# One weight block's last conversion step moved ahead of the next blocks' first step on VectorE, in a fused state-space and GELU kernel

## The chip, the cores and the metric

The kernel runs on one core of a Trainium2 chip. A core has a matrix engine (TensorE; PE in the profile, with its weight loads shown apart as PEld), two elementwise engines (VectorE, DVE in the profile; ScalarE, ACT in the profile), GpSimd (POOL) and SyncE (SP), which mostly starts transfers. Each engine works through its own instructions in order, and waits for others by semaphores. The metric is the device time of one execution in microseconds, lower is better; the time before is the median of three runs.

## The reference, cut to what matters

Two layers follow each other. The first is a chunked state-space scan over 4 sequences of 768 steps with 8 heads; its result is laid out as 3072 tokens of 256 numbers. The second is a two-layer network on these tokens, with a quick GELU between.

```python
    for c in range(nc):                       # chunks of 32 steps; la = log of the clipped a
        cum = np.cumsum(la, axis=-1)
        L = np.exp(cum[:, :, :, None] - cum[:, :, None, :]) * causal
        M = np.einsum('bhin,bhjn->bhij', Cc, Bc) * L
        y[:, :, sl] = np.einsum('bhij,bhjd->bhid', M, xc) \
            + np.einsum('bhin,bhnd->bhid', Cc, state) * np.exp(cum)[:, :, :, None]
        ...                                   # the state is decayed and added to
...
def _moe_ref(x, w_in, w_out) -> np.ndarray:   # x: 3072 x 256
    h = x @ w_in                              # w_in: 256 x 2048
    g = h * (1.0 / (1.0 + np.exp(-1.702 * h)))
    return (g @ w_out).astype(np.float32)     # w_out: 2048 x 256
...
    attn_out = _attn_ref(**attn_kwargs)
    x = np.ascontiguousarray(attn_out.transpose(0, 2, 1, 3)).reshape(B * S, H * D)
    return _moe_ref(x=x, **moe_kwargs)
```

The weights `moe_w_in` and `moe_w_out` are 64-bit floating-point numbers in memory. The kernel reads them as pairs of 32-bit words and makes 32-bit numbers of them itself.

## The kernel before

The 3072 tokens are worked in six groups of 512. For each group the scan gives `yT` (256 features by 512 tokens, two tiles of 128 rows), and the network multiplies it by the 16 column blocks of `w_in` (`w_in[:, f]`, 128 columns each, two halves of 128 rows) and then by the blocks of `w_out`. Group 0 is special: its hidden layer, `hidden(0, f)` for f = 0 to 15, runs while the weights are still being fetched and converted. From group 1 on the weights are all there.

**Conversion.** The weights come in pieces (`PIECES`, line 155): pieces 0 to 3 hold two blocks of `w_in` each, pieces 4 and 5 four blocks each, pieces 6 to 9 four blocks of `w_out` each. So piece 3 is blocks 6 and 7, and piece 4 is blocks 8 to 11. A piece passes through five steps:

- `fetch(i)` (line 164): two transfers from SyncE's queue (line 181).
- `fields(i)` (line 189): two VectorE instructions over the whole piece, which cut the exponent bits into `power[i]` (line 193, tile `p`) and the mantissa bits into `mantissa[i]` (line 196, tile `m`).
- `clamp(i)` (line 199): two ScalarE activations over `power[i]` (lines 204 and 205).
- `rounded(i)` (line 207): one VectorE instruction that adds the low word to the mantissa (line 209).
- `join(i, parts)` (line 216): for each part one VectorE instruction that puts the sign to the power (line 223) and one that multiplies mantissa and power into the weight tile (line 229). With `parts=2` the first half of the piece's blocks is finished before the second.

`narrow(i)` (line 236) orders this on VectorE: `rounded(i)`, then either `join(i)` or `fields(i + 1)` first. For pieces 2, 4, 5 and 6 `join(i)` stands first; for piece 3 `fields(4)` stands ahead of the whole of `join(3, 2)`.

**Hidden layer.** `hidden(g, f)` (line 869) takes a bank of PSUM from a pool of four (`bank`, line 563), issues the two matrix products of the block (line 878; each stands in the profile as two matmuls and two weight loads) and then one activation on ScalarE from that bank into `gT` (line 882). Block f takes the bank that block f - 4 had, so its first product waits for that block's activation.

The order of the program around the change is set by this table and loop; the work listed for f is issued right after `hidden(0, f)`:

```python
    for i, k, c in ((2, 1, 1), (3, 2, 2), (4, 4, 7), (5, 8, 10), (6, 10, 14), (7, 14, 15)):
        at(in_hidden[0], k, lambda i=i: narrow(i))
        at(in_hidden[0], c, lambda i=i: clamp(i + 1))
...
    for f in range(NF):
        hidden(0, f)
        for do in in_hidden[0].get(f, []):
            do()
```

So `narrow(3)` and `clamp(4)` are issued after `hidden(0, 2)`. On ScalarE the two activations of `clamp(4)` therefore stand between the activation of block 2 and that of block 3. `narrow(4)`, which makes blocks 8 to 11, is issued after `hidden(0, 4)`.

Of the kernel before, what the change touches and what calls it, by code (L numbers as in the profile page):

```python
# [35 lines left out]
def kernel(  # L36
# [122 lines left out]
    bits, pieces = {}, {}  # L159

    def words(name):
        return wide.tile([P, 2 * PN], U32, tag="bits", name=name, bufs=BUFS)

    def fetch(i, held=False):
        name, f, n = PIECES[i]
        if n == 2 and f % 4:
            t = pieces.pop(i - 1)[:, 2 * n * DM:]
        else:
            t = pieces[i] = words(f"bits{i}")
            t = t[:, :2 * n * DM]  # L170
        if held:
            held.memset(t[:, :1], 0)
        if name == "in":
            src = moe_w_in[:, 2 * f * P:2 * (f + n) * P].rearrange("(k p) e -> p k e", p=P)
            dst, src = (v.rearrange(s, h=n, e=2 * P) for v, s in (
                (t, "p (h k e) -> k p h e"), (src, "p k (h e) -> k p h e")))
        else:
            src = moe_w_out[f * P:(f + n) * P, :].rearrange("(f p) (h e) -> h p f e", p=P, h=2)
            dst = t.rearrange("p (h f e) -> h p f e", h=2, f=n)
        for k in range(2):  # L180
            nc.sync.dma_start(out=dst[k], in_=src[k])  # L181
        t = t.rearrange("p (e w) -> p e w", w=2)
        bits[i] = t[:, :, 0], t[:, :, 1]
# [3 lines left out]
    mantissa, power = {}, {}  # L187

    def fields(i):
        hi, cols = bits[i][1], slice(0, PIECES[i][2] * DM)  # L190
        mantissa[i] = wide.tile([P, PN], U32, tag="m", name=f"m{i}")[:, cols]
        power[i] = wide.tile([P, PN], U32, tag="p2", name=f"p2{i}")[:, cols]
        nc.vector.tensor_scalar(out=power[i], in0=hi, scalar1=0x7FF00000, scalar2=None,
                                op0=ALU.bitwise_and)

        nc.vector.tensor_scalar(out=mantissa[i], in0=hi, scalar1=0x000FFFFF,
                                scalar2=0x00100000, op0=ALU.bitwise_and, op1=ALU.bitwise_or)
# [9 lines left out]
    def rounded(i):  # L207

        nc.vector.scalar_tensor_tensor(out=mantissa[i].bitcast(FP32), in0=bits[i][0],
                                       scalar=2.0 ** -32, in1=mantissa[i],  # L210
                                       op0=ALU.mult, op1=ALU.add)


    NEXT = {1: (6,), 5: (9,)}

    def join(i, parts=1):

        name, f, n = PIECES[i]
        n //= parts
        low, m, p2 = bits.pop(i)[1], mantissa.pop(i), power.pop(i)  # L220
        for k in range(parts):
            cols, fs = slice(k * n * DM, (k + 1) * n * DM), slice(f + k * n, f + (k + 1) * n)
            nc.vector.scalar_tensor_tensor(out=p2[:, cols], in0=low[:, cols], scalar=0x80000000,
                                           in1=p2[:, cols], op0=ALU.bitwise_and, op1=ALU.bitwise_or)
            if name == "in":
                dst, h = w_in[:, fs].rearrange("p f k e -> p (f k e)").unsqueeze(1), 1
            else:
                dst, h = w_out[:, :, fs].rearrange("p c f e -> p c (f e)"), 2
            nc.vector.scalar_tensor_tensor(  # L229
                out=dst, in0=m[:, cols].bitcast(FP32).rearrange("p (h e) -> p h e", h=h),  # L230
                scalar=2.0 ** -20, in1=p2[:, cols].bitcast(FP32).rearrange("p (h e) -> p h e", h=h),
                op0=ALU.mult, op1=ALU.mult)
        for n in NEXT.get(i, ()):
            fetch(n)

    def narrow(i):
        rounded(i)
        if i in (2, 4, 5, 6):
            join(i, 2 if i in (4, 5) else 1)
        if i == 6:  # L240
            decay_rows(0)
        if i + 1 < len(PIECES):
            fields(i + 1)
        if i not in (2, 4, 5, 6):
            join(i, 2 if i == 3 else 1)


    scratch = dram.tile([NC, 2, NB * NH, H], FP32, name="scratch")
# [133 lines left out]
    for n in range(PG):  # L382
        t = whose[32 * n:32 * n + 32, n:n + 1]
# [115 lines left out]
    def decay_rows(b):  # L499

        t, first = raf.pop(b), firsts.pop(b)
        if b:
            since[b] = ssd.tile([P, NC, P], FP32, tag="since", name=f"since{b}")
        nc.vector.tensor_tensor_scan(
            out=since[b][:, -t.shape[1]:].rearrange("p c s -> p (c s)"), data0=t.rearrange("p c s -> p (c s)"),
            data1=first.rearrange("p c s -> p (c s)"),
            initial=0.0, op0=ALU.mult, op1=ALU.add)
# [686 lines left out]
    dense(8, bank("dense"))  # L1194
    finish(range(PG))
    join(0, 2)
    fold_ident(1)
    fields(1)
# [22 lines left out]
# [3 lines that stand above are left out]
# [3 lines left out]
    n, p = 2 * PG, 3 * PG  # L1227
# [5 lines left out]
       lambda: decay_rows(1))  # L1233
    at(in_project[0], 4, lambda: turn(PG + 1))
    at(in_project[0], 5, lambda: narrow(9))
    at(in_project[0], 10, lambda: score(pairs), lambda: gain(pairs), lambda: keep_both(pairs, True),
       lambda: weigh(PG), lambda: weigh(PG + 1))
# [90 lines left out]
    k = NF // 2 - 1  # L1328
# [6 lines left out]
    for g in range(2, NG):  # L1335
        n, p = (g + 1) * PG, (g + 2) * PG
# [60 lines left out]
        k = NF // 2 - 1  # L1397
# [42 lines left out]
```

## Time and profile before

| | |
|---|---|
| time before, median of 3 runs | 346.89 us (346.83 to 347.21) |
| the profiled execution's own time | 347.67 us |
| its span, first instruction to last | 345.9 us |
| TensorE busy (PE), share of the span | 339.2 us, 98% |
| VectorE busy (DVE) | 256.1 us, 74% |
| ScalarE busy (ACT) | 155.1 us, 45% |
| granted TensorE clock, mean | 1.0 |

A row of the timeline has a start in microseconds from the span's start, a length in microseconds, the engine, the line, the operation, the tile written and the tiles read with their shapes, and how many instructions it merges; a bracket gives the idle time ahead of it on its engine and what ended that. A row of the chain of waits has start, length and what the end of the program hung on then. A row of the list of waits has who waited for whom, the total in microseconds, how often, and the longest. The end of a matmul is modelled. "bits" is the tile of raw words, "p" the power, "m" the mantissa.

### The profile page before, as it was taken

How to read it: one execution, taken by the hardware profiler on the slowest of the kernel's cores; microseconds unless marked ns; L12 is line 12 of the kernel's file. 1: busy time of each engine (PE TensorE's matmuls, PEld its weight loads, DVE VectorE, ACT ScalarE, POOL GpSimd, SP SyncE). 2: the span in 40 equal slices, each digit the busy share in tenths (PEclk: the TensorE clock that was granted, in tenths of full speed). 3: DMA queues.
4: the chain of work that ended last, by engine and by line, in shares of the span. 5: the costliest groups of instructions: out<-in, count | busy, mean ns of one | idle time of the engine just before them, and what ended most of it. 6: DMA issues, size and time to landing. Idle time of an engine off the chain costs nothing.

```text
span 345.9 us, 8116 instructions
## 1 busy us (share of the span) xinstructions
PE 339.2 (98%) x3380; PEld 270.2 (78%) x3380; DVE 256.1 (74%) x484; ACT 155.1 (45%) x352; POOL 16.7 (5%) x40
## 2 busy tenths in 40 slices
PE   8999999999999999999999999999999999999996
PEld 6633744555788888888888888888888888899996
DVE  5988999999799998858995667787564654465463
ACT  5786771507454324754332554442454322554320
POOL 7300110300000100000000000000000000000000
PEclk9999999999999999999999999999999999999999
DMA  6698899545637100435603036400000300000401
GB/s 160 132 289 211 217 239 133 152 67 102 122 63 127 36 0 15 65 99 100 110 27 51 2 78 121 64 0 3 0 4 2 62 2 0 0 2 0 63 0 62
DMA packets 90004, 25.76 MB, mean 74 GB/s; under 512 B 73416, under 2 KB 87248, under 8 KB 89968
## 3 DMA queue, kind: packets, MB, share of 16 engines
q1 hardware_dynamic: 89104, 24.72, 35.0%
q10 hardware_dynamic: 832, 0.52, 0.5%
q8 instruction: 26, 0.43, 0.5%
q14 instruction: 10, 0.08, 0.1%
q0 software_dynamic: 32, 0.01, 0.0%
HBM read 22.00 MB, written 3.24 MB: 73 GB/s over the span
## 4 chain that ended last, share of the span: by engine, by line
PE 92%; DMA 3%; SPq 2%; DVE 1%; issue 0%; ACT 0%; POOL 0%; DVEq 0%
PE acc L1039 28%; PE X L934 19%; PE Y L944 14%; PE o L976 8%; PE acc L1046 7%; PE h L878 7%; DMA bits<-in_moe_w_in_dram 3%; PE y L818 2%; PE cb L664 2%; SPq L181 1%; PE y L804 1%; PE A L695 1%; PE ab L536 1%; DMA az<-in_a_dram 1%; POOL CsT L649 0%
## 5 line engine op out<-in xcount | busy, mean ns | idle before, releaser
L939 ACT ACTIVATE ac<-X 128x256 f32<-128x256 f32 x76 | 29.1, 383 | 81.7 <-PE X L934 81.0
L1039 PE MATMUL acc<-mg,mw 128*128 128x256 f32 x192 | 54.5, 379 | 0.0
L1066 DVE TENSOR_TENSOR gT<-Y,ac 128x512 f32<-128x512 f32 x38 | 26.2, 689 | 38.1 <-PE Y L944 32.5
L911 ACT ACTIVATE gT<-gT 128x512 f32<-128x512 f32 (+1 forms) x76 | 38.9, 519 | 29.3 <-DVE gT L1066 28.8
L934 PE MATMUL X<-my,mi 128*128 128x256 f32 x152 | 45.2, 380 | 0.0
L1039 PEld LDWEIGHTS acc<-mg,mw 128*128 128x128 f32 x192 | 36.6, 190 | 4.9
L1066 DVE TENSOR_TENSOR gT<-Y,b 128x256 f32<-128x256 f32 x38 | 15.8, 419 | 28.5 <-PE Y L944 28.5
L878 PE MATMUL h<-yT,w_in 128*128 128x512 f32 (+1 forms) x92 | 35.5, 541 | 1.4 <-DVE w_in L229 0.9
L1039 PE MATMUL acc<-gT,w_out 128*128 128x256 f32 x128 | 35.5, 380 | 0.0
L878 PEld LDWEIGHTS h<-yT,w_in 128*128 128x128 f32 x92 | 17.2, 190 | 18.2 <-issue 12.8
L934 PEld LDWEIGHTS X<-my,mi 128*128 128x128 f32 x152 | 28.0, 190 | 4.0 <-ACT ac L939 0.3
L976 PE MATMUL o<-gT,w_out 128*128 128x512 f32 x64 | 28.3, 596 | 0.0
L902 DVE TENSOR_TENSOR mg<-gT 128x512 f32<-128x512 f32 x40 | 27.2, 681 | 0.0
L1039 PEld LDWEIGHTS acc<-gT,w_out 128*128 128x128 f32 x128 | 24.3, 190 | 3.4 <-ACT yT L853 0.2
L939 ACT ACTIVATE b<-X 128x256 f32<-128x256 f32 x38 | 14.6, 383 | 20.8 <-PE X L934 20.3
L934 PE MATMUL X<-yT,w_in 128*128 128x256 f32 x76 | 23.2, 389 | 0.0
L944 PE MATMUL Y<-yT,w_in 128*128 128x256 f32 x76 | 22.7, 381 | 0.0
L944 PE MATMUL Y<-my,mi 128*128 128x256 f32 x76 | 22.7, 381 | 0.0
L934 PE MATMUL X<-my,w_in 128*128 128x256 f32 x76 | 22.5, 380 | 0.0
L944 PE MATMUL Y<-yT,mi 128*128 128x256 f32 x76 | 22.5, 380 | 0.0
L976 PEld LDWEIGHTS o<-gT,w_out 128*128 128x128 f32 x64 | 11.9, 190 | 13.6 <-issue 12.7
L408 DVE TENSOR_TENSOR_SCAN L<-a,idents 128x1024 f32<-128x1024 f32 x9 | 20.5, 2279 | 0.3 <-DMA a<-scratch 0.3
(152 smaller groups left out, 547.8 us busy)
## 6 DMA issues: line engine op xcount, KB each, us to landing
a<-scratch SPq DMA_DIRECT2D x18, 256.0 KB, 4.9
bits<-in_moe_w_out_dram SPq DMA_DIRECT2D x8, 512.0 KB, 7.4
x<-in_x_dram SPq DMA_DIRECT2D x24, 128.0 KB, 3.7
out_dram<-ob SPq DMA_DIRECT2D x40, 64.0 KB, 2.0
bits<-in_moe_w_in_dram SPq DMA_DIRECT2D x8, 256.0 KB, 3.7
bits<-in_moe_w_in_dram SPq DMA_DIRECT2D x4, 512.0 KB, 11.4
b<-in_B_dram SPq DMA_DIRECT2D x20, 64.0 KB, 3.3
af<-in_a_dram SPq DMA_DIRECT2D x3, 384.0 KB
```

The costliest lines, as they stand in the source:

```text
L408: nc.vector.tensor_tensor_scan(out=L, data0=ra[p].rearrange("p k e -> p (k e)"), data1=idents.rearrange("p h i -> p (h i)"), initial=0.0, ...
L664: nc.tensor.matmul(out=s["cb"][side, r, k].rearrange("p (q i) -> p q i", q=Q), lhsT=BT[rows, k, side], rhs=CT[rows, k, :, side], start=Tru ...
L878: nc.tensor.matmul(out=h[:, cols], lhsT=w_in[:, f, k], rhs=yT[g][:, k, cols], start=(k == 0 and c == 0), stop=(k == NK - 1), skip_group_ch ...
L902: nc.vector.tensor_tensor(out=t[:, 0:2], in0=B[:, :, 1], in1=B[:, 0], op=ALU.subtract)
L911: nc.scalar.activation(o, i, AF.Silu, scale=GELU_SCALE)
L934: nc.tensor.matmul(out=s["X"], lhsT=lhsT, rhs=rhs, start=i == "1", stop=i == "4", skip_group_check=True)
L939: nc.scalar.activation(copy, s["X"], AF.Copy)
L944: nc.tensor.matmul(out=o, lhsT=lhsT, rhs=rhs, start=s.pop("new", False), stop=i != "5", skip_group_check=True)
L976: nc.tensor.matmul(out=o[c], lhsT=w_out[:, c, f], rhs=gT[g, f // 2][:, f % 2], start=(f == 0), stop=(f == NF - 1), skip_group_check=True)
L1039: nc.tensor.matmul(out=acc[g][0][i][:, cols], lhsT=w, rhs=h[:, cols], start=(j == 0 and k == 0 and (i, 0) in begins), stop=(j == NF // 2 - ...
L1046: nc.tensor.matmul(out=o[k] if type(o) is list else o[:, cols], lhsT=h[:, cols], rhs=w, start=(j == 0 and (i, k) in begins), stop=(j == NF ...
L1066: nc.vector.tensor_tensor(out=o, in0=v, in1=w, op=ALU.add)
```

## The change

In `narrow(3)` the join is taken apart. Before, VectorE had `rounded(3)`, `fields(4)`, `join(3)` for block 6, `join(3)` for block 7. Now it has `rounded(3)`, `join(3)` for block 6, `fields(4)`, `join(3)` for block 7. `join` gets a parameter that names the parts to do, and keeps the piece's tiles until the last part is done. No instruction is added or removed: in the built program the lines 223 and 229 of block 6 (128x256 each) stand ahead of the lines 193 and 196 of piece 4 (128x1024 each) on VectorE, and the order on TensorE, ScalarE, GpSimd and SyncE is as before.

```diff
-    def join(i, parts=1):
+    def join(i, parts=1, only=None):
 
         name, f, n = PIECES[i]
         n //= parts
-        low, m, p2 = bits.pop(i)[1], mantissa.pop(i), power.pop(i)
-        for k in range(parts):
+        low, m, p2 = bits[i][1], mantissa[i], power[i]
+        for k in range(parts) if only is None else only:
             cols, fs = slice(k * n * DM, (k + 1) * n * DM), slice(f + k * n, f + (k + 1) * n)
...
-        for n in NEXT.get(i, ()):
-            fetch(n)
+        if only is None or parts - 1 in only:
+            for t in bits, mantissa, power:
+                t.pop(i)
+            for n in NEXT.get(i, ()):
+                fetch(n)
 
     def narrow(i):
         rounded(i)
...
+        if i == 3:
+            join(i, 2, (0,))
         if i + 1 < len(PIECES):
             fields(i + 1)
-        if i not in (2, 4, 5, 6):
-            join(i, 2 if i == 3 else 1)
+        if i == 3:
+            join(i, 2, (1,))
+        elif i not in (2, 4, 5, 6):
+            join(i)
```

## The prediction, as put on record before the changed kernel ran

> **What bounds the kernel now.** I read the page's chain of waits first, then the chain in order of time around the edit, then the timelines of VectorE, ScalarE and TensorE there, and last the list of waits after it.
>
> ```profile
> PE 92%; DMA 3%; SPq 2%; DVE 1%; issue 0%; ACT 0%; POOL 0%; DVEq 0%
> ...
> 17.15 9.61 DMA bits<-in_moe_w_in_dram
> ...
> 27.28 0.69 DVE p L193
> ...
> 28.95 0.44 DVE w_in L229
> ...
> 29.52 17.43 PE h L878 x52
> ```
>
> The end hangs on TensorE for 92% of the span. The other pieces of the chain lie in the first 29.5 us: the last of them runs from the landing of piece 4's words (17.15 + 9.61 = 26.76) over `fields(4)` and the join of block 6 to TensorE. From 29.52 on TensorE hangs on nothing but itself; of its matmuls after 30 us the list of waits has only the row of this same wait:
>
> ```profile
> PE h L878 <- DVE w_in L229: 0.9, 1, 0.9
> ```
>
> So TensorE's beat set at 29.5 us is carried to the end, and the question is how much earlier it can be. VectorE there:
>
> ```profile
> 25.49 0.69 DVE L209 SCALAR_TENSOR_TENSOR m<-bits,m 128x512 f32<-128x512 uint32 x1
> 27.28 0.69 DVE L193 TENSOR_SCALAR p<-bits 128x1024 uint32<-128x1024 uint32 x1 [1.10 <-DMA bits<-in_moe_w_in_dram]
> 27.89 0.69 DVE L196 TENSOR_SCALAR m<-bits 128x1024 uint32<-128x1024 uint32 x1
> 28.49 0.42 DVE L223 SCALAR_TENSOR_TENSOR p<-bits,p 128x256 uint32<-128x256 uint32 x1
> 28.95 0.43 DVE L229 SCALAR_TENSOR_TENSOR w_in<-m,p 128x256 f32<-128x256 f32 x1
> 29.29 0.42 DVE L223 SCALAR_TENSOR_TENSOR p<-bits,p 128x256 uint32<-128x256 uint32 x1
> ```
>
> Block 6 (lines 223 and 229 at 28.49 and 28.95) stands behind piece 4's fields, and these stand idle 1.10 us for their transfer. ScalarE and TensorE's weight loads:
>
> ```profile
> 25.91 0.72 ACT L205 ACTIVATE p<-p,edge 128x512 uint32<-128x512 f32 x1
> 26.53 0.58 ACT L882 ACTIVATE gT<-h 128x512 f32<-128x512 f32 x1
> 28.01 1.15 ACT L204 ACTIVATE p<-p,edge 128x1024 f32<-128x1024 uint32 x1 [0.90 <-DVE p L193]
> 29.19 1.15 ACT L205 ACTIVATE p<-p,edge 128x1024 uint32<-128x1024 f32 x1
> 30.24 2.04 ACT L882 ACTIVATE gT<-h 128x512 f32<-128x512 f32 x4
> ```
>
> ```profile
> 27.65 0.19 PEld L878 LDWEIGHTS h<-yT,w_in 128*128 128x128 f32 x1 [0.24 <-issue]
> 29.49 0.30 PEld L878 LDWEIGHTS h<-yT,w_in 128*128 128x128 f32 x2 [1.65 <-ACT p L204]
> ...
> 30.89 0.19 PEld L878 LDWEIGHTS h<-yT,w_in 128*128 128x128 f32 x1 [0.24 <-ACT gT L882]
> ...
> 32.75 0.47 PEld L878 LDWEIGHTS h<-yT,w_in 128*128 128x128 f32 x2 [0.38 <-issue]
> ```
>
> Two things are to be seen. The load at 27.65 is block 5's last; at a beat of 0.43 the next would come at 28.08, and comes at 29.49. And the load at 30.89, block 7's first, is released by an activation of line 882: block 7 takes the PSUM bank of block 3, whose activation is the first of the four at 30.24, behind `clamp(4)`, which waits for piece 4's line 193. It ends at 30.24 + 0.58 = 30.82. In the kernel before, TensorE comes to block 7 just as that bank is freed. That is a second gate right behind the first, and the edit doesn't move it forward.
>
> **The change, part by part.** Nothing is added or removed; two pairs of VectorE instructions change places. No transfer is issued by either, and no queue but VectorE's is reordered.
>
> *Block 6 forward.* Line 223 of block 6 waits for `clamp(3)`'s line 205, which ends at 25.91 + 0.72 = 26.63; after such an end it starts 0.03 later (the same timelines: line 205 at 22.61 for 0.72, line 223 at 23.36, for piece 2): 26.66. Line 229 follows 0.46 later (28.49 to 28.95), at 27.12, and ends at 27.55. TensorE's load follows 0.11 after such an end (29.38 to 29.49), at 27.66, before the beat of 28.08. So the wait at block 6 goes. Its price: after a wait the second load of a block follows the first by 0.11 (two loads of 0.19 in 0.30), so block 6's second load is at 29.60 before; on the beat it would be at 28.08 + 0.43 = 28.51. Gain at block 6: 1.09 us.
>
> *Fields of piece 4 back.* Line 193 waits for the landing (27.28 before) and now also for line 229 of block 6. After a line 229 of 128x256 the next instruction starts 0.34 later (28.95 to 29.29): 27.12 + 0.34 = 27.46. So it moves from 27.28 to 27.46, 0.18 later. This place is not in the trace; the lower bound is 27.28 (the landing alone), the upper is the full row of line 229 and 0.03, 27.58. I take 27.46, since a line 193 behind a 128x512 line 229 also starts before that row's end (piece 1's line 229 is at 20.79 for 0.69, to 21.48; the line 193 behind it at 21.40).
>
> [...]
>
> *What is late next.* `clamp(4)`'s lines 204 and 205, then the activations of blocks 3 to 6, stand behind that line 193 on ScalarE, all 0.18 later: block 3's ends at 30.82 + 0.18 = 31.00. TensorE, now early, would load block 7 at 28.08 + 4 × 0.43 = 29.80, and stands until the bank is free. The release comes 0.05 us after the activation (block 0's load at 18.44, after line 838 ended at 17.18 + 1.21 = 18.39) to 0.11 (above): first load 31.05 to 31.11, second 31.16 to 31.22. Before, block 7's second load was 29.60 + 4 × 0.43 = 31.32. So block 7 is 0.10 to 0.16 earlier; I take 0.13.
>
> *Cover behind it.* Block 7's own weights end at 27.46 + 0.61 + 0.60 + 0.46 + 0.43 = 29.56, long before. Line 209 of piece 4 moves from 30.09 to 29.46 (two short joins less behind the fields), line 223 of block 8 from 31.22 to 29.46 + 1.13 = 30.59 (line 205 ends at 30.34 + 0.18 = 30.52, so it isn't held), and the weights of blocks 8 and 9 are there 0.63 earlier (line 229 at 31.94 for 0.69 before): 32.63 - 0.63 = 32.00. TensorE wants them at about 32.47 (second load 31.19 + 4 × 0.43 = 32.91, first 0.43 ahead). If this cover of 0.36 us were gone, all of the 0.13 would go with it. Banks of blocks 4 to 6 are freed 0.51 apart after block 3's, faster than TensorE's 1.72 a block.
>
> Sum: 1.09 gained at block 6, 0.96 given back at block 7, net 0.13 us gain, carried to the end. Against the profiled execution: span 345.9 - 0.13 = 345.77, and with the 1.77 around the span 347.54. That execution was 0.78 above the median; on the median it is 346.89 - 0.13 = 346.76, say 346.8.
>
> **The rivals.** Changes of under 0.2%, 0.69 us, are what a measurement of this kernel can't tell from none; its three runs lie 0.38 apart.
>
> *Slower: the words of piece 4 land earlier in ordinary executions.* The price is all in the 0.18: before, everything starts with the landing; after, line 193 can't come before 27.46. If the landing is d earlier than in this execution, the change costs d - 0.13. It decides from d = 0.13 on. For it: the profiled execution is 0.78 longer than the median, and the transfer is a queue of 14.6 us (12.65, the first of these issues, to 27.28). Against: a proportional share of the 0.78 is 0.78 × 14.6 / 347 = 0.03. If all 0.78 lie there, the time is 346.89 + 0.65 = 347.5. The end of this scale is line 209's end at 26.18: d at most 1.1, loss 0.97, 347.9.
>
> *Much faster: block 7 isn't held by the bank.* Then block 8's weights are the next limit: at 32.00 + 0.11 first load and 0.11 more, 32.22, against 31.32 + 1.72 = 33.04 before: 0.82 gain, 346.1. For it: before, that load at 30.89 is on TensorE's own beat too (29.49, 29.60, then 0.43 each), so no lost time shows the wait. Against: the row names the activation as the releaser, and four banks make block 7 the heir of block 3.
>
> *The landing is later.* Then line 193 isn't delayed at all, and the gain is 0.13 + 0.18 = 0.31: 346.6.
>
> *The change doesn't do what it says.* If VectorE ran in the old order, 346.9. The built order has the swap and nothing else, so little is left for it.
>
> **How the numbers follow.** Forecast, within 0.3 us of before: 0.73. Early landing with a loss over 0.3: 0.14, half of it over 0.69. No hold by the bank: 0.04. Late landing: 0.05. No swap: 0.02. Something later in the program that turns the small advance into a wait of its own: 0.02. Gains and losses share the forecast's middle, so its own range is 346.6 to 347.2; the range of 8 in 10 goes to 346.4 below (beyond it only the bank's absence) and to 347.5 above (the early landing with all the 0.78). Faster by over 0.2% is the bank's case and a little, 0.05; slower by over 0.2% half of the early landing and the later wait, 0.09; the rest, 0.86, lies within.
>
> **What would show it right or wrong.** Right: lines 223 and 229 of block 6 at about 26.66 and 27.12 on VectorE; line 193 right behind, with no idle time put to the transfer; block 6's first load at 28.08 with no wait; a new gap of about 1.25 us ahead of block 7's first load, at about 31.1, released by line 882; the TensorE run that begins at 29.52 before now broken there. Wrong: block 7 loaded at about 29.8, or line 193 still ended by the transfer, or a TensorE gap after 33 us that the kernel before doesn't have. A change over 0.69 us either way refutes the sum.

## The result, and the profile after

| | before | changed |
|---|---|---|
| median of 21 runs each | 346.83 us (346.43 to 348.52) | 347.72 us (347.40 to 348.04) |
| ratio to before, 95% interval | 1 | 1.0019 (1.0011 to 1.0028) |
| profiled execution: time, span | 347.67, 345.9 us | 347.89, 346.2 us |

The change makes the kernel slower, by 0.11 to 0.28% in the ratio of the means, and by 0.89 us in the medians. The 21 times of before fall into two groups, fourteen from 346.43 to 347.21 and seven from 347.61 to 348.52; the times of the changed kernel all lie above the lower one. The profiled execution of before, 347.67 us, on which the prediction was built, belongs to the upper group. In the three later batches the 73 times of before show no such gap, but run on from 346.33 to 347.64, with four more above; their medians, given below, are much the same. Of all 94 times 12 lie above 347.60, so an execution as slow as the profiled one is the less usual case.

In the changed kernel the chain of waits in order of time (start, length, what it hung on) no longer comes from a transfer. It runs through VectorE's and ScalarE's conversion, and TensorE enters it at block 7:

```profile
26.99 0.44 DVE p L223
...
27.79 0.70 DVE p L193
28.49 0.02 issue
28.52 1.16 ACT p L204
29.68 0.02 issue
29.70 1.15 ACT p L205
30.85 0.49 ACT gT L889
31.34 0.04 issue
31.38 15.75 PE h L885 x48
```

Lines past 213 are seven higher than before: 885 is the old 878, 889 the old 882. The same stretch on VectorE, and TensorE's weight loads (start, length, engine, line, and in brackets the idle time ahead and its releaser):

```profile
25.81 0.69 DVE L209 SCALAR_TENSOR_TENSOR m<-bits,m 128x512 f32<-128x512 uint32 x1
26.99 0.43 DVE L223 SCALAR_TENSOR_TENSOR p<-bits,p 128x256 uint32<-128x256 uint32 x1 [0.49 <-ACT p L205]
27.45 0.42 DVE L229 SCALAR_TENSOR_TENSOR w_in<-m,p 128x256 f32<-128x256 f32 x1
27.79 0.69 DVE L193 TENSOR_SCALAR p<-bits 128x1024 uint32<-128x1024 uint32 x1
```

```profile
21.86 0.30 PEld L885 LDWEIGHTS h<-yT,w_in 128*128 128x128 f32 x2 [0.98 <-DVE w_in L229]
...
28.40 0.19 PEld L885 LDWEIGHTS h<-yT,w_in 128*128 128x128 f32 x1 [0.24 <-issue]
...
31.38 0.30 PEld L885 LDWEIGHTS h<-yT,w_in 128*128 128x128 f32 x2 [1.50 <-ACT gT L889]
```

The load at 21.86 is block 2's first, which waits for the weights of piece 1. Block 6's pair stands ahead of line 193; block 6's first load, at 28.40, is on the beat; TensorE's loads stand idle for 1.50 us ahead of block 7's first, until block 3's activation frees the bank. That is the picture the prediction drew. What it got wrong is what this is to be compared with: how the kernel before usually runs.

### The profile page after: what moved, and what is told of

Its sections match the earlier page's. It is cut to its first block, busy times and chain, and to the rows that moved or that the text cites. A ratio compares the mean times of both kernels' runs of the same rounds, so it can differ in the third digit from the quotient of the medians.

```text
span 346.2 us, 8116 instructions
## 1 busy us (share of the span) xinstructions
PE 340.4 (98%) x3380; PEld 270.5 (78%) x3380; DVE 255.8 (74%) x484; ACT 155.3 (45%) x352; POOL 17.1 (5%) x40
## 4 chain that ended last, share of the span: by engine, by line
PE 93%; DVE 3%; ACT 2%; issue 1%
PE acc L1046 28%; PE X L941 19%; PE Y L951 14%; PE o L983 8%; PE acc L1053 7%; PE h L885 7%; PE cb L671 2%; PE y L825 2%; PE y L811 1%; PE A L702 1%; ACT p L204 1%; ACT p L205 1%; PE ab L543 1%; PE busy L457 1%; DVE p L223 1%
```

## The experiments

Every run is compared with runs of the kernel before on the same chip in the same batch; their medians were 346.95, 346.84 and 346.94 us in the three batches below.

### The kernel before, looked at again

No edit; two more profiled executions.

> The unchanged kernel, profiled once more. Landing theory (piece 4's words usually land about 1 us earlier than in the first profile, so block 6 is not late in the kernel before and the edit only pushes line 193 back): an execution of about 346.6 us has line 193 of piece 4 right behind line 209, at about 26.2 us, not ended by the transfer, and no wait at block 6's weight load; one of about 347.8 us looks like the first profile, with line 193 ended by the transfer at about 27.3. Start theory (what differs lies ahead of 13 us, in how long TensorE's first matmuls stay slow): an execution of 346.6 us still has line 193 ended by the transfer and block 6 late by 1.1, and its gain lies ahead of 13 us.

> The unchanged kernel, profiled a third time. Landing theory: as in the expectation of the second profile, line 193 of piece 4 right behind line 209 where the time is under 347.1, ended by the transfer where block 6 is late.

They took 347.02 and 346.95 us, with spans of 345.3 and 345.2. VectorE and TensorE in the third profile of before:

```profile
25.75 0.69 DVE L209 SCALAR_TENSOR_TENSOR m<-bits,m 128x512 f32<-128x512 uint32 x1
26.37 0.68 DVE L193 TENSOR_SCALAR p<-bits 128x1024 uint32<-128x1024 uint32 x1
```

```profile
18.30 27.83 PE L878 MATMUL h<-yT,w_in 128*128 128x512 f32 x76 [0.51 <-ACT yT L838]
```

Line 193 follows line 209 after 0.62 us with no idle time: piece 4's words are already there. In the first profile there were 1.10 us idle, ended by the transfer. TensorE's 76 matmuls of the hidden layer are one run, with no row that waits at block 6 or 7. The first loads of block 2 and of block 6 in that profile:

```profile
21.80 0.30 PEld L878 LDWEIGHTS h<-yT,w_in 128*128 128x128 f32 x2 [0.62 <-DVE w_in L229]
...
28.56 0.40 PEld L878 LDWEIGHTS h<-yT,w_in 128*128 128x128 f32 x2 [0.46 <-ACT p L204]
```

Block 6's second load, at 28.56 + 0.40 - 0.19 = 28.77, comes two beats of 0.43 after block 5's last (27.91): nothing is lost there. The second profile has line 193 at 26.64, again right behind line 209 at 26.03. From the start of the hidden layer to the transposes that end it these two executions take 45.97 - 18.30 = 27.67 and 46.24 - 18.37 = 27.87 us; the first profile took 46.79 - 17.89 = 28.90, the changed kernel 46.97 - 18.00 = 28.97. Part of these differences lies ahead of the edit, in the wait for block 2's weights. From block 2's first load to the transposes both executions take 24.17 us (45.97 - 21.80 and 46.24 - 22.07), the first profile 46.79 - 21.53 = 25.26, the changed kernel 46.97 - 21.86 = 25.11. So against these two executions the change costs 0.94 us here, and 0.9 to 1.0 us of span. The start theory falls: the second profile is later than the first one up to 26 us (line 229 of piece 2 at 24.63 against 24.09) and still ends 0.6 us sooner.

### Fetching piece 5 later, to hasten piece 4

```diff
-    for i in range(2, 6):
+    for i in range(2, 5):
         fetch(i)
     nc.sync.dma_start(out=az[:BH].rearrange("p c s -> p (c s)"),
                       in_=a.rearrange("b h s -> (b h) s"))
     spread_rows(0)
+    fetch(5)
```

> The kernel before with piece 5 (blocks 12 to 15) fetched behind the two small transfers of a instead of ahead of them, so that piece 4 has the transfer engines to itself. Landing theory: all executions near the fast ones of before, 346.4 to 346.9 us, none near 347.8, and line 193 of piece 4 not ended by a transfer. Start theory: two clusters of times stay, near 346.6 and 347.8.

> The changed kernel with the same reordering of fetches. Landing theory: line 193 waits for block 6's pair and not for the transfer, so nothing changes: 347.5 to 348.0 us, about 1.0 us above the kernel before with the same reordering. Start theory: the same times as the kernel before with this reordering, within 0.3 us.

In the kernel before it missed: 347.92 us in the median of eleven (346.83 to 350.18; one more took 354.23), ratio 1.0030 (1.0011 to 1.0048). In the profiled execution the edit didn't do what it was for, as VectorE shows:

```profile
26.97 0.69 DVE L193 TENSOR_SCALAR p<-bits 128x1024 uint32<-128x1024 uint32 x1 [0.79 <-DMA bits<-in_moe_w_in_dram]
```

Piece 4 was still late in that execution (347.26 us), though piece 5 was issued behind two other transfers. Why other executions took over 348 was not found. In the changed kernel the same edit gave 347.57 (347.32 to 350.4): as expected, nothing moved, and its line 193 at 27.53 is not ended by a transfer. This pair doesn't decide between the theories, since it didn't make piece 4 land early.

### Taking the landing away

Piece 4's conversion reads the words of pieces 2 and 3; the weights of blocks 8 to 11 are not those of the reference.

```diff
+        if i == 2:
+            landed.append(pieces[2].rearrange("p (e w) -> p e w", w=2))
+        if i == 4:
+            t = landed[0]
         bits[i] = t[:, :, 0], t[:, :, 1]
```

> The kernel before, but the conversion of piece 4 reads the words of pieces 2 and 3, which have landed by about 25 us, instead of its own (blocks 8 to 11 of w_in get wrong values; the transfer of piece 4 still runs). Landing theory (the landing of piece 4 differs between executions and is all that separates the kernel's times): line 193 of piece 4 starts right behind line 209 in every execution, block 6 is not late, and the times are one cluster at the fast end of before, 346.4 to 346.9 us. Rival (the times of before differ for another reason, for instance the first matmuls): the same spread of times as before, 346.4 to 347.5.

> The changed kernel with the same false source for piece 4. Landing theory: line 193 waits for the pair of block 6 anyway, so the times are those of the changed kernel, 347.4 to 348.0 us, and 0.9 to 1.0 us above the kernel before with the same false source; in the profile block 6 is on the beat and block 7's first load waits about 1.3 us for the activation of block 3. Rival: the same time as the kernel before with the false source, within 0.3 us.

In the order of before: 346.85 us, eight of twelve runs from 346.47 to 346.94, four from 347.46 to 348.00. In the order of the change: 347.64 (347.32 to 347.91). The difference of 0.79 us without any wait for piece 4 is the cost of the new order by itself; from block 2's first load to the transposes the two profiles differ by 46.72 - 21.62 = 25.10 less 45.69 - 21.52 = 24.17, 0.93 us. But there are still upper times, so the landing is not its only cause. The execution that was profiled, 347.46 us, was one of these, and it lost time further on. TensorE there:

```profile
82.19 0.47 PE L699 MATMUL A<-x,Be 64*32 64x64 f32 x32
82.85 0.35 PE L699 MATMUL A<-x,Be 64*32 64x64 f32 x16 [0.18 <-DVE my L906]
83.59 0.32 PE L699 MATMUL A<-x,Be 64*32 64x64 f32 x8 [0.39 <-DMA x<-in_x_dram]
```

Its hidden layer ended at 45.69, earlier than in any profile above, and at 82 us TensorE waited 0.18 us for VectorE and 0.39 us for a transfer of x that had not landed; no profile of the unedited kernel has these waits. So a second limit can lie behind the first, where an early TensorE loses its lead.

### Making the landing late

```diff
+    rest = []
+    for i in range(4, 6):
+        fetch(i, rest=rest)      # the second half's transfer goes into rest
+    for do in rest:
+        do()
```

> The kernel before with the four transfers of pieces 4 and 5 interleaved (first half of 4, first half of 5, second half of 4, second half of 5), so that piece 4 is complete about 1 us later, after 28 us. Landing theory: line 193 is ended by the transfer in every execution, block 6 waits for it, and the time is 0.5 to 2 us above the kernel before. Rival: no change beyond 0.3 us.

> The changed kernel with the same interleaving. Landing theory: both kernels now start piece 4's line 193 at the landing, so nothing is pushed back, and the changed kernel is FASTER than the unchanged one with this interleaving, by 0.27 to 0.33 us: the sign of the change turns round. Rival: still slower than the unchanged one with this interleaving, by the same 0.7 to 0.9 us as without it.

Order of before: 348.83 us (348.00 to 349.51, six runs). Order of the change: 348.14 (347.99 to 348.41, five). The medians turn round, by 0.69 us, but with so few runs the intervals of the two ratios to before overlap (1.0038 to 1.0069, 1.0025 to 1.0050), so the profiles have to show the sign. The lines 196 here are the old 193; VectorE in the order of before, then of the change:

```profile
27.80 0.69 DVE L196 TENSOR_SCALAR p<-bits 128x1024 uint32<-128x1024 uint32 x1 [1.48 <-DMA bits<-in_moe_w_in_dram]
```

```profile
27.35 0.42 DVE L232 SCALAR_TENSOR_TENSOR w_in<-m,p 128x256 f32<-128x256 f32 x1
28.01 0.69 DVE L196 TENSOR_SCALAR p<-bits 128x1024 uint32<-128x1024 uint32 x1 [0.24 <-DMA bits<-in_moe_w_in_dram]
```

Both now wait for the transfer. Block 7's second load was at 31.83 and at 31.71, though line 196 started 0.21 later in the second: at an equal start of that line the change gains 0.12 + 0.21 = 0.33 us, the top of what was expected. That the medians differ by more may come from the landing, which differs between executions; it isn't shown.

### The bank: clamp(4) behind block 3's activation

```diff
-    for i, k, c in ((2, 1, 1), (3, 2, 2), (4, 4, 7), (5, 8, 10), (6, 10, 14), (7, 14, 15)):
+    for i, k, c in ((2, 1, 1), (3, 2, 3), (4, 4, 7), (5, 8, 10), (6, 10, 14), (7, 14, 15)):
```

> The changed kernel with the two activations of clamp(4) behind the activation of block 3 on ScalarE instead of ahead of it. If block 7 waits for block 3's bank (the gate of the prediction): block 7's load on the beat, the next limit is the weights of block 8, 0.65 us gained over the changed kernel, about 347.1 us. Start theory: nothing gained, 347.7 us.

> The kernel before with clamp(4) behind the activation of block 3, which takes that activation's bank out of the question. Landing theory: with an early landing the clamp comes 0.5 us later than before and block 8 waits about 0.2 us; with a late one block 6 waits as before. Times like the kernel before or 0.1 to 0.2 us above it, 346.8 to 347.1 in the median; the moved clamp is worth something only in the changed kernel. Rival (the moved clamp is good by itself): 0.5 us faster than the kernel before.

In the changed kernel: 347.22 us (346.88 to 349.74), 0.5 below the changed kernel's 347.72, near the 0.65 expected (against before in the same batch it is 0.27 above, the changed kernel was 0.89 above); the ratio, 1.0013 (0.9996 to 1.0029), doesn't tell it from before. ScalarE and the loads of its profile:

```profile
26.83 1.07 ACT L889 ACTIVATE gT<-h 128x512 f32<-128x512 f32 x2
28.48 1.15 ACT L204 ACTIVATE p<-p,edge 128x1024 f32<-128x1024 uint32 x1 [0.58 <-DVE p L193]
```

```profile
30.10 0.19 PEld L885 LDWEIGHTS h<-yT,w_in 128*128 128x128 f32 x1 [0.24 <-issue]
...
32.42 0.30 PEld L885 LDWEIGHTS h<-yT,w_in 128*128 128x128 f32 x2 [0.85 <-ACT gT L889]
```

The activation of block 3 now stands in the gap ahead of the clamp, and block 7 is loaded at 30.10 on the beat; the wait has gone on to block 8, whose weights are ready at 31.61 + 0.69 = 32.30. The row names an activation, but that of block 4, whose bank block 8 takes, is the first of three that start at 30.72 and take some 0.5 us each, long done by then. So the bank was the gate. (The execution profiled took 347.55 us, at the upper end of its runs.) In the kernel before the same move gave 346.89 (346.61 to 347.37), ratio 1.0002 (0.9993 to 1.0010): nothing, since that gate is hardly shut there (in the third profile of before block 7's first load stands idle for 0.30 us, against 0.24 on the beat).

### Block 7's pair moved ahead too

```diff
         if i == 3:
-            join(i, 2, (0,))
+            join(i, 2)
```

with the second half's join behind the fields taken out.

> The changed kernel with the join of both blocks 6 and 7 ahead of the fields of piece 4. Bank theory: line 193 of piece 4 comes 0.79 us later (0.45 + 0.34 for the second pair), the activation of block 3 and block 7's first load 0.79 us later as well: 348.4 to 348.6 us, 0.8 above the changed kernel. Rival (the changed kernel's loss has another place): the same time as the changed kernel, 347.7 us.

348.37 us (348.20 to 348.46, four runs), ratio 1.0044 (1.0030 to 1.0058), 0.65 above the changed kernel: just under the range expected. In its profile line 193 is at 28.61 and block 7's first load at 32.20, both 0.82 later than in the changed kernel. In the profile the work put ahead of line 193 arrives in full at block 7; why the times show somewhat less was not found.

### Removing both waits

The moved clamp, and the join of piece 4 in four parts, so that block 8 is ready earlier.

```diff
-            join(i, 2 if i in (4, 5) else 1)
+            join(i, {4: 4, 5: 2}.get(i, 1))
```

> The changed kernel with clamp(4) behind the activation of block 3 (as in the run before with that alone) and with the join of piece 4 in four parts instead of two, so that block 8's weights are ready 0.5 us earlier. Bank theory: neither block 7 nor block 8 waits, TensorE is on its beat from block 6 to the end of the hidden layer whether piece 4 lands early or late; 346.5 to 346.9 us, 0.3 less than with the moved clamp alone, 0.8 less than the changed kernel, and no executions near 347.8. Rival (a wait further on, for the tokens x at about 83 us, takes what is gained here): not below 347.1 us.

347.75 us (347.27 to 348.24), ratio 1.0023 (1.0014 to 1.0032): missed, no better than the changed kernel. TensorE in its profile:

```profile
18.22 28.16 PE L885 MATMUL h<-yT,w_in 128*128 128x512 f32 x76 [0.51 <-ACT yT L845]
...
65.49 0.30 PE L702 MATMUL A<-x,Be 64*32 64x64 f32 x2
66.38 0.78 PE L702 MATMUL A<-x,Be 64*32 64x64 f32 x54 [0.60 <-DVE CsT L656]
```

The hidden layer is one unbroken run and ends at 46.21, 0.76 before the changed kernel's. But at 65.5 TensorE now waits for VectorE, which the four further instructions of the join have made late: line 656 is at 65.91 here, 65.12 with the moved clamp alone. Most of these 0.79 us is accounted for: 0.22 are a delay that this execution had before (line 193 of piece 4 at 27.98 against 27.76, line 229 of piece 2 at 24.60 against 24.39) and 0.52 come between that line and the fields of piece 5 (34.29 against 33.55). From the first of the A products to the next run of line 983 TensorE takes 67.09 - 65.49 = 1.60 us, in the third profile of before 65.96 - 65.24 = 0.72. What was gained at block 7 was lost there. No kernel tried here beats the one before.

## Why the prediction was wrong, step by step

The profiles of the runs above can be put side by side in one measure that starts ahead of the edit's place: from block 2's first load, how long until piece 4's first step (the old line 193) starts, and how long until the transposes that end the hidden layer.

| one profiled execution each | piece 4's first step | end of the hidden layer |
|---|---|---|
| order of before: second and third profile | 4.57 us | 24.17 us |
| order of before, landing taken away | 4.56 us | 24.17 us |
| order of before, piece 5 fetched later | 5.44 us | 24.94 us |
| order of before: first profile | 5.75 us | 25.26 us |
| order of before, landing made late | 6.13 us | 25.64 us |
| order of the change | 5.93 us | 25.11 us |
| order of the change, landing taken away | 5.93 us | 25.10 us |
| order of the change, piece 5 fetched later | 5.92 us | 25.10 us |
| order of the change, landing made late | 6.25 us | 25.43 us |
| block 7's pair moved ahead too | 6.72 us | 25.90 us |

Where that step came late, the hidden layer ended 19.50 to 19.51 us after it in the order of before, and 19.17 to 19.18 us after it in the order of the change. That is the gain of 0.33 us. But the new order didn't start the step before 5.92 us, and the old one, when the words were there, started it at 4.57 and lost nothing. So the change cost 0.94 us then, and by these rows it would gain only where the old order starts the step later than 25.11 - 19.51 = 5.60 us.

- *Order on VectorE and the price at line 193: right.* Line 193 follows line 229 after 0.34 us (27.45 to 27.79), as worked out, and starts 0.08 before that row's end, here 27.45 + 0.42 = 27.87. The prediction's upper bound, the full row and 0.03, would be 27.90 here; the start lies 0.11 ahead of it. All of this stretch is 0.32 later than in the first profile, since the execution was (line 229 of piece 2 at 24.41 against 24.09).
- *Block 6 on the beat, block 7 held by block 3's bank: right.* The load follows the activation's end, 30.75 + 0.58 = 31.33, by 0.05 us, inside the 0.05 to 0.11 taken. The moved clamp shows the gate: with it, block 7's wait is gone.
- *"If this cover of 0.36 us were gone": right.* Block 8's weights are ready at 32.34 and its load comes at 32.78, with no wait.
- *Gain at block 6, 1.09 us: wrong term.* It is true of the first profile and of no other profile of before: in the second and the third block 6 was not late, so there was nothing to gain, while the 0.96 us at block 7 are paid all the same (0.94 measured from block 2's load). Against the first profile alone the sum holds: 0.13 us of gain less the 0.21 by which the conversion started later relative to the hidden layer (0.32 less 0.11) gives a loss of 0.08; measured 28.97 - 28.90 = 0.07.
- *The step that failed* is in the first rival: "a proportional share of the 0.78 is 0.03". The profiled execution was 0.78 us above the median of its runs, and the prediction spread that over the whole span instead of asking which wait could hold it. The largest wait in the chain that depended on a transfer, 1.10 us, was the very one the edit acted on. The rival had the mechanism, the sign and the cap of 0.97 us (0.94 us found in the hidden layer, 0.9 to 1.0 us of span); it was given 0.14. Its price at "all 0.78" was 347.5 and at the end of its scale 347.9; the measured median is 347.72, and in both later profiles the words had landed before VectorE could use them, which is that end of the scale. All that the prediction named as signs of being right came true, some 0.3 us later than given; they look at the changed kernel alone, and none of them at how the kernel before usually runs.
- *The other rivals:* the bank does hold block 7, so the much faster case is out. The case of a later landing was made by hand, and its two profiles show the gain of about 0.3 us that was named for it.

What stays open: how often piece 4 is late in unprofiled executions of before, and which of its upper times come from that and which from the x transfer at 83 us. Three profiles of before can't say. Nor was it found what sets the landing; with piece 5 issued later, piece 4 was late all the same in the one execution profiled.

## What to carry to other kernels

Before a wait for a transfer is costed from one profile, compare the profiled execution's time with the other runs: if it is slow by about the size of that wait (here 0.78 us, and a wait of 1.10), the wait may be missing from most executions, and an edit that reorders work around it pays its price for nothing. Follow what the instruction that is pushed back feeds: here a delay of 1.36 us on VectorE (4.57 to 5.93 in the table) went over two ScalarE steps to an activation that frees a PSUM bank, and the block that was made early only reached that wait sooner. Where several engines run close behind each other, removing one wait with extra instructions can move the limit to the engine that got them: here four more on VectorE took 0.52 us, and TensorE stood idle for 0.60 us until its line 656 was done.

## What the runs showed of the hardware

The landing of the same transfers, issued in the same order by the same program, differed between executions: line 193 of piece 4 was held until 27.28 in one profile of before, and was free by 26.37 and 26.64 in two others.

Between the end of that transfer in the chain of waits and the start of the VectorE row that waited for it lay 0.52 us in the first profile of before (26.76 to 27.28), 0.52 with piece 5 fetched later (26.45 to 26.97), 0.50 in the order of before with the landing made late (27.30 to 27.80), and 0.10 in the order of the change with it (27.91 to 28.01). What makes the difference is not shown.

TensorE's early products don't always take the same time. Rows of the first 32 matmuls of line 536 (543 in the changed kernel), in the first profile of before and in the changed kernel's:

```profile
5.66 0.69 PE L536 MATMUL ab<-cum,pick 32*64 32x128 f32 x32 [0.30 <-DVE cum L346]
```

```profile
5.78 1.16 PE L543 MATMUL ab<-cum,pick 32*64 32x128 f32 x32
```

The same work took 0.69 and 1.16 us, 1.7 times as long, while the granted clock of that stretch reads 1.00 in both. So the granted clock as the profile gives it doesn't tell the two apart, and no run here shows what does.
